# Sums of weights at a fixed place of each step, second weights ahead of first ones, one count of conversion pieces for each place

## The chip, the cores and the metric

One core of a Trainium2 chip runs the kernel. Times are device microseconds (us) of one launch. The engines are TensorE (PE; its weight loads are PEld), VectorE (DVE), ScalarE (ACT), GpSimd (POOL) and SyncE (SP), which issues the DMAs. Each engine runs its own instructions in order, and semaphores hold an instruction until what it needs is there.

## The reference, cut to what matters

Attention with a learned bias feeds two blocks of matrix products. The change lies in the second half of the first block:

```python
def _moe_ref(x, w_tok1, w_tok2, w_ch1, w_ch2):      # x: (4, 576, 512)
    xt = x.transpose(0, 2, 1)
    h = np.maximum(xt @ w_tok1, 0.0) @ w_tok2        # 576 -> 256 -> 576
    u = x + h.transpose(0, 2, 1)
    h2 = np.maximum(u @ w_ch1, 0.0) @ w_ch2          # 512 -> 1536 -> 512
    return (u + h2).astype(np.float32)
```

The second block has weights w_in (512 x 1024) and w_out (512 x 512). All these weights arrive as 64-bit floats.

## The kernel before, in words

The channel products `u @ w_ch1` and `h2 @ w_ch2` run over 2304 token columns. The 1536 hidden units are cut into 12 rows f of 128, and the rows into six pairs j. Weight row f of w_ch1 is called c1 f here (first weights), row f of w_ch2 is c2 f (second weights).

Two passes go over the columns, `d0` and `d1` (class `Double`), each over 1024 columns in two blocks of 512; `d0` takes the 256 columns left over with it (`up256`, `down256`). In a pass, `run` makes one step n for each pair j. A step does the first product by a scheme with seven small products in the place of eight: P1, b, S2, S1, S3, P4 and S4, of six matmuls each, some of which use sums of weights (`wsum`, tile ws). Then come the second products, `down`, 12 matmuls each. Products for the left block run in each step (`down1`), those of the right block only once a group of two pairs is through: a step with n = 2 or 4 "begins" a group, closes the last one (four adds to X, L1277) and runs four more `down` (in `other`). Two result buffers `gs` pass the hidden values from ACT (high part, L1111) and DVE (low part, L1115) to PE. Every operand is a pair of a high and a low part, and a product takes three matmuls: high by high, high by low, low by high.

Weights are brought into that form on the chip by a queue of jobs (class `Jobs`). A job takes a 512 KB weight tile in four pieces, each one DVE instruction (L161, L171, L179, L185), with one square on ACT (L158); a piece of the next job also issues the job's high part (ACT, L122) and low part (DVE, L132). SP loads the tile of the next job as a job starts; two tiles of raw weights are held. `work(k)` issues up to k pieces, as long as `wjobs.limit` allows it, and `step` calls `work`; these calls are the places. `wjobs.need(key)` issues all pieces that a weight still needs, at once. The sums are jobs too: ("raw", j) makes four differences (L989, two steps), ("sum", j) makes the high part (L992, ACT), the low part (L995, DVE), and stores tiles to DRAM for pass `d1` (`keep`).

Before, the queue holds for each j: c1 2j, c1 2j+1, raw j, sum j, c2 2j, c2 2j+1. In `d0` a place has 3 pieces (`pieces`), with none at the first two places of a step that begins; the limit rises at marked points (`hooks0`). The token products of the stage before `d0` have their own counts (TP0, TP1, TPD), 26 pieces in all. Behind the product b stands `wjobs.need(("sum", j))`; in front of `down256` stands `wjobs.need(("c2", f))`. At the start of `d0` pieces are issued until sum 1 is done.

All code is written in the order in which it is to run; nothing reorders it.

Of the kernel before, what the change touches and what calls it, by code (L numbers as in the profile page):

```python
# [19 lines left out]
def kernel(ctx, tc, ins, consts, out, dbg=None, nb=4, stop=None):  # L20
# [30 lines left out]
    NF = CH // P  # L51
# [876 lines left out]
    D1 = C256 + CS  # L928
# [48 lines left out]
    S1, S3, S4, S2 = range(4)  # L977
    summed, sum_room = set(), []

    def sum_steps(j):  # L980

        def w(f):
            t = wjobs.last["c1", f].rearrange("p (a b) -> p a b", a=ND)
            return t[:, 0:ND2], t[:, ND2:ND]

        raw = []

        def add(i, x, y, op=ALU.subtract):
            V.tensor_tensor(out=raw[0][:, i], in0=x, in1=y, op=op)  # L989

        def hi(o):
            S.copy(out=wsum[j][:, 0, o], in_=raw[0])  # L992

        def lo(o):
            V.tensor_tensor(out=wsum[j][:, 1, o], in0=raw[0], in1=wsum[j][:, 0, o].bitcast(F32), op=ALU.subtract)  # L995

        def sums(first, second):
            (a11, a12), (a21, a22) = w(2 * j), w(2 * j + 1)
            if first:
                add(0, a21, a22, ALU.add)  # L1000
                add(1, a11, a21)
            if second:
                k = len(raw[0].shape) and raw[0].shape[1] - 2
                add(k + 1, raw[0][:, 0], a11)
                add(k, a12, raw[0][:, k + 1])

        def kept_():
            wjobs.subtract()
            if j < NJ - 2:
                keep("a", j, wa[j])  # L1010
                keep("b", j, wb[j])

        def done():
            if j < NJ - 1:
                keep("s", j, wsum[j])
            summed.add(j)

        def small_one():
            wjobs.finish()
            new_s(j)  # L1020
            raw.append(stg.tile([P, WMAX], F32, tag="sq", name="sq").rearrange("p (o a b) -> p o a b", o=2, a=ND2))
            sums(True, False)
            hi(slice(0, 2))

        def small_two():
            lo(slice(0, 2))
            sums(False, True)
            hi(slice(2, 4))

        def small_three():  # L1030
            lo(slice(2, 4))
            done()

        def one():
            raw.append(sum_room[0].rearrange("p i (o a b) -> p (i o) a b", o=2, a=ND2))
            sums(True, False)

        def two():
            sums(False, True)

        def three():
            new_s(j)
            hi(slice(0, 4))

        def four():
            lo(slice(0, 4))
            done()

        if j == 0:
            return [lambda: None], [small_one, small_two, small_three, kept_]  # L1050
        if j == 1:
            return [one, two], [three, four, wjobs.finish, kept_]
        return [one, two], [wjobs.finish, three, kept_, four]

    def c1_jobs(j):
        for f, dst in ((2 * j, a_dst), (2 * j + 1, b_dst)):
            fs = slice(f * P, (f + 1) * P)
            wjobs.add(("c1", f), "moe_w_ch1", slice(0, DM), fs, ND, lambda dst=dst: dst(j))
        raws_, sums_ = sum_steps(j)
        wjobs.add_steps(("raw", j), raws_)  # L1060
        wjobs.add_steps(("sum", j), sums_)

    base = len(wjobs.queue)
    for j in range(NJ):
        c1_jobs(j)
        for f in (2 * j, 2 * j + 1):
            fs = slice(f * P, (f + 1) * P)
            wjobs.add(("c2", f), "moe_w_ch2", fs, slice(0, DM), 1, lambda f=f: [[t[:, :] for t in c2[f]]])
    wjobs.limit = base + 8
    wjobs.load()  # L1070

    def work(k):
        for _ in range(k):
            if wjobs.gen is not None or wjobs.next < min(len(wjobs.queue), wjobs.limit):
                wjobs.piece()
# [51 lines left out]
    if True:  # L1127
        TP0, TP1, TPD = 2, 1, (2, 2, 1, 1)
        M2, M1 = mixers
# [21 lines left out]
        for b in range(nb):  # L1151
            if b == nb - 1:
                u = u_parts(0, u0)
            if b > 0:
                h = new_h()
                work(TP0)
                for m in range(NTT):
                    if m == 1 and b + 1 < nb:
                        work(TP1)
                    ph = pk["h"].tile([P, DM], F32, tag="h", name="ph")  # L1160
                    tok1(xs, m, ph)
                    tok1_out(ph, m, h)
# [8 lines left out]
            for d in range(ND):  # L1171
# [6 lines left out]
                if b == nb - 1 and d == 2:  # L1178
                    x256 = chw.tile([P, 2, ND, CS], F32R, tag="ws1", name="x256")
                    split(X[:, :, C256:C256 + CS], x256[:, 0], x256[:, 1])  # L1180
                work(0 if b == nb - 1 else TPD[d])
    tk.release()
# [74 lines left out]
    with tc.tile_pool(name="ps_ch", bufs=1, space=PSUM, reuse_waits="tile") as pc:  # L1257
# [30 lines left out]

        def step(k):
            work(k)  # L1290
            rfill(1)
# [39 lines left out]
        class Double:  # L1331
# [29 lines left out]

            def other(self, acc, lst, k, n=0):
                down(acc, self.g(k), lst[k][0], k == 0, k == len(lst) - 1)
                if k + 2 < len(lst):
                    self.second(k + 2, lst)
                step(n)

# [26 lines left out]
            def run(self, hooks, first=False, small=False, banks=("ma", "ma", "mb", "mb"), end=None, fill=None):  # L1394
# [3 lines left out]
                for n, (group, j) in enumerate(seq):  # L1398
# [11 lines left out]
                    sm, da = small and n < len(seq) - 1, n > 0 and not (first and n == 1)  # L1410
                    k_ = self.pieces
                    k1 = 0 if begins and small else k_
                    a = bank(banks[n % 2])
                    product(a, self.half(w_a, 0), self.half(self.u, 0), start=True)
                    S.copy(out=s1, in_=a)
                    step(k1)
                    two = da and not sm and not begins
                    if da:
                        self.down1(pj, 0, pgrp, range(ND2) if two else range(ND))
                    step(k1)  # L1420
                    if begins:
# [11 lines left out]
                    hooks(n, "P2")  # L1433
                    wjobs.need(("sum", j))
                    product(a, ws_(S2), M2)
                    S.copy(out=c12, in_=a)
                    step(k_)
                    if two:
                        self.down1(pj, 0, pgrp, range(ND2, ND))
                        relu(s1, gs[0])  # L1440
                    if sm:
                        up256(j)
                        hooks(n, "up")
                        step(k_ if not begins else 1)
                        relu_lo_256()
                    if begins:
                        acc = new_acc()
                        self.other(acc, lst, 0, k_)
                        if not small:
                            self.other(acc, lst, 1, k_)  # L1450
                    c = bank(banks[3] if sm else "mx")
# [7 lines left out]
                    hooks(n, "P7")  # L1459
                    step(k_)  # L1460
                    if begins:
                        for k in range(1 if small else 2, len(lst)):
                            self.other(acc, lst, k, k_ if k + 1 < len(lst) else 0)
                            if not small and k == len(lst) - 2:
# [5 lines left out]
                    elif n > 0:  # L1470
                        self.down1(pj, 1, pgrp)
                        step(1)
                    elif fill is not None:
# [12 lines left out]
                    if not small:  # L1486
                        step(1)
                group, j = seq[-1]
# [7 lines left out]
                else:  # L1496
                    self.second(0, lst)
                    step(self.pieces)
                self.down1(j, 1, group)
# [4 lines left out]
                self.second(1, lst)  # L1504
                step(self.pieces)
                acc = [bank(nm) for nm in end] if end else new_acc()
                for k in range(len(lst) - 1):
                    self.other(acc, lst, k, self.pieces)
                    build()
# [29 lines left out]
        d1 = Double(D1, [order1[i:i + 2] for i in range(0, NJ, 2)])  # L1539
        d0.pieces, d1.pieces = 3, 0  # L1540
        scratch = rp_.tile([P, 2, DM], F32, tag="r", name="scratch")
# [5 lines left out]
        def hooks0(n, where):  # L1547
            if where == "start":
                wjobs.limit = base + 6 * (n + 1) + 1
                if n == 0:  # L1550
                    wjobs.limit = base + 10
                    while 1 not in summed:
                        wjobs.piece()
                    mixer(3, raws(), 0)
            if n == 1 and where == "P2":
                mixer(4, raws(), 0)
            if where == "up":
                wjobs.limit = base + 6 * (n + 1) + (3 if n > 0 else 4)
            if n == 0 and where == "others":
# [3 lines left out]
            if n == 0 and where == "C21":  # L1563
                work(2)
                mixer(1, slots[2:4], 0)
            if where == "P3":
                wjobs.limit = base + 6 * (n + 1) + 6
                work(4 if n > 0 else 0)
            if n < NJ - 1:
# [12 lines left out]
        def hooks1(n, where):  # L1582
# [10 lines left out]
            if where == "done":  # L1593
# [6 lines left out]
                wjobs.load()  # L1600
                d1.pieces = 2
            if n == NJ - 1 and where == "P4":
# [335 lines left out]
```

## Time and profile before

| | |
|---|---|
| median of 3 runs | 886.04 us (884.84 to 886.21) |
| the profiled execution | 884.93 us, span 883.1 us |
| PE busy | 853.7 us, 97% of the span |
| DVE busy | 696.8 us, 79% |
| ACT busy | 454.8 us, 51% |
| mean granted clock of PE | 0.988 |

Times within the trace count from the start of the span. The profiled execution takes 1.8 us more than its span. PE's busy time includes matmuls that run at a lower clock. In views by windows a row gives the stretch and its length, then the busy time and instruction count of PE, PEld, DVE, ACT and POOL, the granted clock of PE, the DMA share and GB/s. In views of waits a row gives who waited for whom, the total in us, how often, and the longest. In a timeline the bracket is the idle time before the instruction and what ended it.

### The profile page before, as it was taken

What the parts mean: (1) busy time and instruction counts of PE and PEld (TensorE: products, weight loads), DVE (VectorE), ACT (ScalarE), POOL (GpSimd) and SP (SyncE); (2) the same over time, 40 slices, a digit from 0 to 9 for tenths busy, and PEclk for the clock granted to TensorE, in tenths of its full rate; (3) what the DMA queues carried; (4) which work ended last, traced back from release to release, by engine and by line L of the source; (5) the groups of instructions that cost most, each with busy time, mean ns of one, the idle gap of its engine ahead of it and who ended that gap; (6) DMA issues with size and microseconds to landing.
All of it is one profiled execution on the core that took longest, in us unless ns stands there. A gap on an engine that the chain in (4) does not pass through costs nothing.

```text
span 883.1 us, 21618 instructions
## 1 busy us (share of the span) xinstructions
PE 853.7 (97%) x8608; PEld 708.4 (80%) x8608; DVE 696.8 (79%) x1521; ACT 454.8 (51%) x992; POOL 231.4 (26%) x440
## 2 busy tenths in 40 slices
PE   8999999999999999997897899999999999999998
PEld 4466788888888988886686778888878989989997
DVE  7899788888887778895785696556579889988756
ACT  7999888888888534442332343213244432323310
POOL 1345567666676100000000000000003332322230
PEclk9999999999999999998998999999999999999999
DMA  7966543444432132232341202326025001010002
GB/s 189 192 137 135 141 82 75 82 89 92 94 69 56 50 112 91 96 104 111 96 155 71 72 1 72 106 109 212 27 85 115 25 1 49 1 60 1 1 13 96
DMA packets 127733, 74.30 MB, mean 84 GB/s; under 512 B 104593, under 2 KB 112913, under 8 KB 126353
## 3 DMA queue, kind: packets, MB, share of 16 engines
q1 hardware_dynamic: 127472, 72.79, 31.4%
q8 instruction: 68, 1.11, 0.6%
q14 instruction: 33, 0.26, 0.1%
q10 hardware_dynamic: 160, 0.13, 0.1%
HBM read 47.01 MB, written 13.11 MB: 68 GB/s over the span
## 4 chain that ended last, share of the span: by engine, by line
PE 53%; DVE 8%; ACT 2%; issue 1%; DVEq 0%
PE a L1269 12%; PE ps L1749 6%; PE pu L1727 6%; PE po L1780 6%; PE pv L1674 6%; PE ma L1105 5%; PE mx L1105 2%; PE my L1105 2%; PE mb L1105 2%; PE mx L1301 2%; DVE X L1277 1%; PE ph L684 1%; PE pu L1140 1%; DVE g L1115 1%; PE mx L1322 1%; PE my L1322 1%
## 5 line engine op out<-in xcount | busy, mean ns | idle before, releaser
L540 POOL TENSOR_SCALAR pr<-pr,sm 128x576 f32<-128x576 f32 (+2 forms) x208 | 130.2, 643 | 45.9 <-DVE sm L533 37.7
L1269 PE MATMUL a<-g,c 128*128 128x512 f32 x528 | 125.9, 390 | 0.0
L1269 PEld LDWEIGHTS a<-g,c 128*128 128x128 f32 x528 | 98.6, 188 | 21.4 <-DVE g L1115 1.0
L526 ACT ACTIVATE pr<-pr,mn 128x576 f32<-128x576 f32 x144 | 112.2, 780 | 6.6 <-DVE mn L513 4.4
L513 DVE CUSTOM_DVE_ANT_0 pr<-ss,bias_m 128x576 f32<-128x576 f32 x128 | 94.5, 749 | 18.9 <-PE ss L507 17.1
L63 POOL TENSOR_TENSOR y<-X,y 128x576 fp32r<-128x576 f32 x4 | 6.6, 1690 | 375.4 <-DMA wsr<-in_moe_w_sg_dram 375.4
L607 PEld LDWEIGHTS o<-xA,vm 64*64 64x64 f32 x1280 | 69.8, 133 | 11.1 <-issue 5.4
L607 PE MATMUL o<-xA,vm 64*64 64x128 f32 (+1 forms) x1280 | 78.7, 261 | 0.0
L1224 DVE STREAM_TRANSPOSE res<-X 32x256 f32<-32x256 f32 (+1 forms) x176 | 68.2, 387 | 2.8
L608 PE MATMUL o<-yA,vm 64*64 64x128 f32 x1024 | 67.7, 272 | 0.0
L507 PE MATMUL ss<-kt,X 64*64 64x288 f32 x816 | 66.8, 410 | 0.0
L608 PEld LDWEIGHTS o<-yA,vm 64*64 64x64 f32 x1024 | 56.2, 133 | 0.4
L1749 PE MATMUL ps<-wsT,vn 128*128 128x288 f32 x384 | 56.5, 295 | 0.0
L384 DVE TENSOR_SCALAR X<-ttab,wsm 128x576 f32<-128x576 f32 x108 | 55.3, 572 | 0.1
L1749 PEld LDWEIGHTS ps<-wsT,vn 128*128 128x128 f32 x384 | 52.7, 188 | 0.5 <-DVE tmp L1757 0.2
L1727 PEld LDWEIGHTS pu<-y,c 128*128 128x128 f32 x384 | 51.3, 188 | 0.3
L1727 PE MATMUL pu<-y,c 128*128 128x288 f32 x384 | 51.5, 294 | 0.0
L583 PE MATMUL x<-ident,pr 128*128 128x128 f32 x320 | 47.0, 273 | 0.0
L1780 PE MATMUL po<-u,gm 128*128 128x512 f32 x192 | 44.0, 389 | 0.0
L158 ACT ACTIVATE sq<-wraw 128x512 f32<-128x512 f32 (+2 forms) x44 | 28.8, 654 | 28.8 <-DVE w L185 18.4
L1111 ACT ACTIVATE g<-cs 128x512 fp32r<-128x512 f32 x24 | 15.2, 632 | 52.6 <-PE a L1269 36.8
L63 POOL TENSOR_TENSOR gm<-uT,gm 128x512 fp32r<-128x512 f32 x16 | 23.7, 1482 | 69.8 <-ACT gm L62 69.8
(262 smaller groups left out, 2004.6 us busy)
## 6 DMA issues: line engine op xcount, KB each, us to landing
wraw<-in_moe_w_ch_dram SPq DMA_DIRECT2D x24, 512.0 KB, 3.5
bias_m<-bst SPq DMA_DIRECT2D x32, 288.0 KB, 3.9
s<-ws SPq DMA_DIRECT2D x5, 1024.0 KB, 4.2
ws<-s SPq DMA_DIRECT2D x5, 1024.0 KB, 5.2
vm<-in_v_dram SPq DMA_DIRECT2D x32, 128.0 KB, 3.3
wraw<-in_moe_w_in_dram SPq DMA_DIRECT2D x8, 512.0 KB, 4.9
out_dram<-res SPq DMA_DIRECT2D x16, 256.0 KB, 2.1
kr<-in_k_dram SPq DMA_DIRECT2D x48, 72.0 KB, 2.6
```

Of the source, the lines that this page charges most:

```text
L507: T.matmul(ss[a % na][o, hf, 0:HN], lhsT=ql, rhs=kr_, start=True, stop=True)
L513: V.tensor_tensor_reduce(out=pr[:, a * NB:a * NB + N].rearrange("p (f n) -> p f n", f=2), in0=ss[a][:, :, 0:HN], in1=bias[a].rearrange("p ...
L526: S.activation(out=pr[:, a * NB:a * NB + N], in_=pr[:, a * NB:a * NB + N], func=AF.Exp, scale=-1.0, bias=mn[:, a:a + 1], accum_out=sm[:, a ...
L540: G.tensor_scalar(out=pr[:, dc:dc + hi - lo], in0=pr[:, lo:hi], scalar1=sm[:, a:a + 1], scalar2=1.0, op0=ALU.mult, op1=ALU.mult,)
L607: T.matmul(o[0:HD, 0:w], lhsT=vm[r, t, 0], rhs=xs[r, t, 0:w], start=st_, stop=en)
L608: T.matmul(o[HD:P, 0:w], lhsT=vm[r, t, 1], rhs=rh[r], start=st_, stop=en)
L1105: T.matmul(ps, lhsT=w[i][:, d], rhs=x[j][:, d], start=start and d == 0 and n == 0, stop=stop and d == ND2 - 1 and n == 2, skip_group_check ...
L1224: V.transpose(out=o, in_=src(c)[32 * a:32 * a + 32])
L1269: T.matmul(acc[d], lhsT=c2[f][i][:, d * P:(d + 1) * P], rhs=g[:, j], start=start and m == 0, stop=stop and m == 2,)
L1727: T.matmul(pu[:, hf, 0:HN], lhsT=wi[i][0][d][:, f * P:(f + 1) * P], rhs=y[j][:, d, js], start=d == 0 and m == 0, stop=d == ND - 1 and m == 2,)
L1749: T.matmul(ps[:, hf, 0:HN], lhsT=vn[i][:, t, ds_], rhs=wsT[j][:, t, js], start=t == 0 and m == 0, stop=False,)
L1780: T.matmul(po[:, cs], lhsT=g[i][:, d, gs], rhs=wo[j][d][:, cs], start=d == 0 and m == 0, stop=d == NG - 1 and m == 2,)
```

## The change: what it does

It changes four things in the order of the instructions.

1. The queue. The jobs for c2 of pair j stand in front of those for c1 of pair j (from j = 1). "raw" remains a job; the job "sum" becomes "kept", which only finishes the low parts and stores them.
2. The sums. For n > 1 their high part is issued at a new hook behind P1 (behind ACT's copy s1), their low part and the store at a new hook behind the first `down1`. For j = 1 both come at the start of `d0`. `wjobs.need(("sum", j))` goes. For j = 0 they are part of the job "raw".
3. The counts. `work()` takes its count from a list of 115, one for each call. The places and their order stay. The list gives 30 pieces to the token stage, and pieces to the first two places of the steps that begin.
4. The limits follow the new order of the queue.

```diff
-        def three():
+        def whole():
             new_s(j)
             hi(slice(0, 4))

-        def four():
+        def rest_():
             lo(slice(0, 4))
             done()

         if j == 0:
-            return [lambda: None], [small_one, small_two, small_three, kept_]
-        if j == 1:
-            return [one, two], [three, four, wjobs.finish, kept_]
-        return [one, two], [wjobs.finish, three, kept_, four]
+            return [small_one, small_two, small_three], [kept_]
+        sums_of[j] = whole, rest_
+        return [one, two], [wjobs.finish, kept_]
...
     for j in range(NJ):
-        c1_jobs(j)
+        if j == 0:
+            c1_jobs(j)
         for f in (2 * j, 2 * j + 1):
             wjobs.add(("c2", f), ...)
+        if j > 0:
+            c1_jobs(j)
+    at = {job[0]: i + 1 for i, job in enumerate(wjobs.queue)}
-    wjobs.limit = base + 8
+    wjobs.limit = at["c1", 3]
...
-    def work(k):
-        for _ in range(k):
+    counts = [
+        2, 2, 1, 2, 1, 1, 2, 3, 1, 2, 2, 1, 3, 2, 1, 1, 2, 0, 1, 0, 0, 1, 0, 4,
+        3, 3, 3, 4, 1, 3, 2, 0, 3, 0, 4, 3, 3, 1, 0, 4, 1, 3, 6, 2, 3, 3, 3, 0,
+        2, 4, 0, 2, 3, 0, 2, 2, 6, 4, 0, 3, 4, 4, 1, 1, 4, 1, 6, 0, 0, 0, 0, 0,
+        1, 0, 0, 0, 0, 2, 0, 0, 0, 0, 0, 0, 0, 0, 0, 0, 4, 2, 3, 2, 0, 0, 0, 3,
+        2, 2, 2, 3, 2, 0, 0, 1, 1, 2, 4, 1, 1, 1, 1, 1, 2, 4, 1,
+    ]
+    def work():
+        for _ in range(counts.pop(0)):
             if wjobs.gen is not None or wjobs.next < min(len(wjobs.queue), wjobs.limit):
                 wjobs.piece()
...
                     S.copy(out=s1, in_=a)
-                    step(k1)
+                    hooks(n, "P1")
+                    step()
...
                         self.down1(pj, 0, pgrp, range(ND2) if two else range(ND))
-                    step(k1)
+                    hooks(n, "D1")
+                    step()
...
                     hooks(n, "P2")
-                    wjobs.need(("sum", j))
...
             if where == "start":
-                wjobs.limit = base + 6 * (n + 1) + 1
+                wjobs.limit = at["c1", min(2 * n + 2, NF - 2)]
                 if n == 0:
-                    wjobs.limit = base + 10
-                    while 1 not in summed:
-                        wjobs.piece()
+                    wjobs.limit = at["raw", 1]
+                    wjobs.need(("raw", 1))
+                    for f in sums_of[1]:
+                        f()
                     mixer(3, raws(), 0)
+            if n > 1 and where in ("P1", "D1"):
+                if where == "P1":
+                    wjobs.need(("raw", n))
+                sums_of[n][where == "D1"]()
...
             if where == "up":
-                wjobs.limit = base + 6 * (n + 1) + (3 if n > 0 else 4)
+                wjobs.limit = at["c1", 2 * n + 4] if 2 * n + 4 < NF else at["kept", NJ - 1]
...
             if where == "P3":
-                wjobs.limit = base + 6 * (n + 1) + 6
-                work(4 if n > 0 else 0)
+                work()
```

Every other `work(k)` and `step(k)` loses its argument in the same way.

## Rows read from the trace of the kernel before

**Rows 1.** The page, part 2: busy tenths in 40 slices.
```profile
PE   8999999999999999997897899999999999999998
...
PEclk9999999999999999998998999999999999999999
```

**Rows 2.** Waits of PE from 358 to 545 us.
```profile
PE ma L1105 <- DVE ws L995: 8.3, 2, 4.4
PE my L1322 <- DVE c L132: 3.5, 4, 1.6
PE my L1322 <- ACT c L122: 2.6, 4, 0.9
```

**Rows 3.** Busy time by windows: last token batch, then d0's steps 0 to 5.
```profile
342.93:358.61 15.68, 15.68 (x91) 13.94 (x89) 13.59 (x21) 8.85 (x15) 0.00 (x0) 1.00 0.11 34
358.61:377.43 18.82, 17.40 (x98) 14.80 (x97) 15.90 (x27) 8.77 (x15) 0.00 (x0) 1.00 0.35 127
377.43:396.10 18.67, 18.42 (x104) 15.68 (x103) 18.24 (x32) 9.31 (x18) 0.00 (x0) 1.00 0.33 92
396.10:442.03 45.93, 37.15 (x164) 30.12 (x163) 29.74 (x52) 11.72 (x21) 0.00 (x0) 0.89 0.31 106
442.03:462.96 20.93, 20.93 (x114) 18.25 (x115) 17.63 (x30) 8.46 (x14) 0.00 (x0) 1.00 0.49 164
462.96:509.96 47.00, 37.58 (x163) 30.19 (x161) 29.59 (x52) 12.39 (x22) 0.00 (x0) 0.89 0.20 67
509.96:525.05 15.09, 15.09 (x66) 12.50 (x67) 13.87 (x24) 8.19 (x14) 0.00 (x0) 1.00 0.01 1
```

**Rows 4.** Busy time by windows, behind the longest wait of step 2.
```profile
409.60:414.00 4.40, 4.37 (x16) 3.98 (x17) 2.40 (x4) 1.16 (x2) 0.00 (x0) 0.50 0.68 276
414.00:418.00 4.00, 4.00 (x25) 3.56 (x24) 0.69 (x1) 0.60 (x1) 0.00 (x0) 1.00 0.42 131
```

**Rows 5.** Timeline of step 2 around that wait.
```profile
404.09 0.69 DVE L1115 SCALAR_TENSOR_TENSOR g<-cs,g 128x512 fp32r<-128x512 f32 x1 [4.24 <-ACT g L1111]
...
404.70 2.48 DVE L1277 TENSOR_TENSOR X<-a,X 128x512 f32<-128x512 f32 x4
...
408.36 1.22 DVE L995 TENSOR_TENSOR ws<-scratch,ws 128x1024 fp32r<-128x1024 f32 x1
...
409.63 2.08 PE L1105 MATMUL ma<-m,ws 128*128 128x512 f32 x4 [4.43 <-DVE ws L995]
```

**Rows 6.** Groups by line from 285 to 540 us: busy, mean ns.
```profile
L179 DVE SCALAR_TENSOR_TENSOR w<-wraw,w 128x512 int32<-128x512 int32 x24 | 16.6, 690 | 0.7
...
L161 DVE TENSOR_SCALAR w<-wraw 128x512 int32<-128x512 int32 x24 | 10.1, 419 | 0.0
...
L132 DVE TENSOR_TENSOR c<-w,c 128x512 fp32r<-128x512 f32 x12 | 8.2, 686 | 1.7 <-ACT c L122 1.7
...
L995 DVE TENSOR_TENSOR ws<-scratch,ws 128x1024 fp32r<-128x1024 f32 x5 | 6.1, 1221 | 2.1 <-ACT ws L992 2.1
...
L992 ACT CAST ws<-scratch 128x1024 fp32r<-128x1024 f32 x5 | 5.2, 1048 | 17.8 <-issue 9.4 <-DVE scratch L989 8.4
```

**Rows 7.** Timeline at the start of d0.
```profile
364.92 1.05 ACT L992 CAST ws<-scratch 128x1024 fp32r<-128x1024 f32 x1 [8.44 <-DVE scratch L989]
...
369.12 0.59 ACT L1381 ACTIVATE cs<-ma 128x512 f32<-128x512 f32 x1
...
374.57 1.58 PE L1322 MATMUL my<-g,c 128*128 128x256 f32 x11 [0.53 <-DVE g L1115]
```

**Rows 8.** Timeline in the second token batch.
```profile
325.60 0.63 PE L668 MATMUL px<-ident,X 128*64 128x128 f32 x4 [1.61 <-DVE x L63]
```

**Rows 9.** The tile wraw from 285 to 540 us.
```profile
DMA to landing us min/median/max: 3.3/3.5/4.3
```

**Rows 10.** Timeline where d1 ends and the second block begins.
```profile
667.54 6.63 POOL L63 TENSOR_TENSOR y<-X,y 128x576 fp32r<-128x576 f32 x4 [375.43 <-DMA wsr<-in_moe_w_sg_dram]
...
667.72 1.93 DVE L132 TENSOR_TENSOR c<-w,c 128x512 fp32r<-128x512 f32 x1
```

More of the change, by code (lines that the diff above doesn't have):

```diff
@@ L977 @@
     S1, S3, S4, S2 = range(4)
-    summed, sum_room = set(), []
+    sums_of, sum_room = {}, []
     def sum_steps(j):
@@ L1015, in done @@
                 keep("s", j, wsum[j])
-            summed.add(j)
         def small_one():
@@ L1060, in c1_jobs @@
         wjobs.add_steps(("raw", j), raws_)
-        wjobs.add_steps(("sum", j), sums_)
+        wjobs.add_steps(("kept", j), sums_)
     base = len(wjobs.queue)
     for j in range(NJ):
-        c1_jobs(j)
+        if j == 0:
+            c1_jobs(j)
         for f in (2 * j, 2 * j + 1):
@@ L1127 @@
     if True:
-        TP0, TP1, TPD = 2, 1, (2, 2, 1, 1)
         M2, M1 = mixers
@@ L1155 @@
                 h = new_h()
-                work(TP0)
+                work()
                 for m in range(NTT):
                     if m == 1 and b + 1 < nb:
-                        work(TP1)
+                        work()
                     ph = pk["h"].tile([P, DM], F32, tag="h", name="ph")
@@ L1180 @@
                     split(X[:, :, C256:C256 + CS], x256[:, 0], x256[:, 1])
-                work(0 if b == nb - 1 else TPD[d])
+                work()
     tk.release()
@@ L1287, in relu, with step @@
             relu_lo(src, g)
-        def step(k):
-            work(k)
+        def step():
+            work()
             rfill(1)
@@ L1360, in g, with other @@
                 return gs[(k + self.small) % 2]
-            def other(self, acc, lst, k, n=0):
+            def other(self, acc, lst, k):
                 down(acc, self.g(k), lst[k][0], k == 0, k == len(lst) - 1)
@@ L1365, in other @@
                     self.second(k + 2, lst)
-                step(n)
+                step()
             def pair0(self):
@@ L1410, in run @@
                     sm, da = small and n < len(seq) - 1, n > 0 and not (first and n == 1)
-                    k_ = self.pieces
-                    k1 = 0 if begins and small else k_
                     a = bank(banks[n % 2])
@@ L1419, in run @@
                         self.down1(pj, 0, pgrp, range(ND2) if two else range(ND))
-                    step(k1)
+                    hooks(n, "D1")
+                    step()
                     if begins:
@@ L1433, in run @@
                     hooks(n, "P2")
-                    wjobs.need(("sum", j))
                     product(a, ws_(S2), M2)
                     S.copy(out=c12, in_=a)
-                    step(k_)
+                    step()
                     if two:
@@ L1443, in run @@
                         hooks(n, "up")
-                        step(k_ if not begins else 1)
+                        step()
                         relu_lo_256()
@@ L1447, in run @@
                         acc = new_acc()
-                        self.other(acc, lst, 0, k_)
+                        self.other(acc, lst, 0)
                         if not small:
-                            self.other(acc, lst, 1, k_)
+                            self.other(acc, lst, 1)
                     c = bank(banks[3] if sm else "mx")
@@ L1459, in run @@
                     hooks(n, "P7")
-                    step(k_)
+                    step()
                     if begins:
                         for k in range(1 if small else 2, len(lst)):
-                            self.other(acc, lst, k, k_ if k + 1 < len(lst) else 0)
+                            self.other(acc, lst, k)
                             if not small and k == len(lst) - 2:
@@ L1471, in run @@
                         self.down1(pj, 1, pgrp)
-                        step(1)
+                        step()
                     elif fill is not None:
@@ L1486, in run @@
                     if not small:
-                        step(1)
+                        step()
                 group, j = seq[-1]
@@ L1497, in run @@
                     self.second(0, lst)
-                    step(self.pieces)
+                    step()
                 self.down1(j, 1, group)
@@ L1504, in run @@
                 self.second(1, lst)
-                step(self.pieces)
+                step()
                 acc = [bank(nm) for nm in end] if end else new_acc()
                 for k in range(len(lst) - 1):
-                    self.other(acc, lst, k, self.pieces)
+                    self.other(acc, lst, k)
                     build()
@@ L1539 @@
         d1 = Double(D1, [order1[i:i + 2] for i in range(0, NJ, 2)])
-        d0.pieces, d1.pieces = 3, 0
         scratch = rp_.tile([P, 2, DM], F32, tag="r", name="scratch")
@@ L1563, in hooks0 @@
             if n == 0 and where == "C21":
-                work(2)
+                wjobs.limit = at["c1", 4]
+                work()
                 mixer(1, slots[2:4], 0)
             if where == "P3":
-                wjobs.limit = base + 6 * (n + 1) + 6
-                work(4 if n > 0 else 0)
+                work()
             if n < NJ - 1:
@@ L1600, in hooks1 @@
                 wjobs.load()
-                d1.pieces = 2
             if n == NJ - 1 and where == "P4":
```

## Prediction

> **What bounds the kernel now.** I read the page first: PE is busy nearly throughout, and the two dips in its slices are also the only ones in its clock [rows 1]. Then the waits of PE over the pass d0: the sums of weights (ws, L995) and the second weights (c, from L132 and L122) head them, and each of the largest falls in two places only [rows 2]. Then windows cut at the starts of d0's steps [rows 3]. The reader is to see there that steps 3 and 5 are PE from end to end, at full clock, while steps 2 and 4, which begin a group, take 45.93 and 47.00 us at a clock of 0.89.
>
> What would those two take without a wait? Step 5 is 66 matmuls of 512 columns in 15.09 us, 0.229 us each. Step 3 is 20.93 us. A beginning step is step 3 and four more `down` of 12 matmuls: 20.93 + 48 x 0.229 = 31.9 us. So step 2 loses 14.0 us and step 4 15.1 us, 29.1 us in all. That is the most that these steps can give back.
>
> The timeline of step 2 shows how [rows 5]. The first two places of a beginning step have no pieces, so DVE sits idle for 4.24 us; then the low part g, four adds to X and last the low part of the sums go through its queue, and PE waits 4.43 us at S2. [...] Later in the same step `down256` finds its c2 weights unconverted; all that is left of them is issued in front of it.
>
> **The new order, counted.** The queue, the limits and the counts of the diff fix which piece falls on which place, and so do those of the kernel before. Counted out, two things follow. No `need` has to force a piece inside d0 any more; before, the sums of pairs 2 and 4 and five second weights were forced. And the DVE work that each step issues (instructions by their durations: a conversion 0.42 + 3 x 0.69, a low part 0.69, the low sum 1.22 [rows 6], an add to X 0.62 [rows 5]) becomes: step 0 17.0 to 18.6 us, step 1 21.8 to 23.5, step 2 29.8 to 29.0, step 3 20.4 to 21.7, step 4 29.8 to 28.6, step 5 13.8 to 7.4. The count for step 2 before, 29.8, stands against 29.74 us of DVE in its window [rows 3]. DVE instructions that don't depend on each other follow at about 0.62 (four adds in 2.48 us), so the work of steps 2 and 4 fits in 31.9 us of PE, with little over.
>
> **Steps 2 and 4: the sums.** ACT's high sum costs 1.05 us and stands behind the copy s1, at P1's end; DVE's low sum costs 1.22 us. Counted from the start of step 2: P1 ends at 1.4; DVE still has the tail of step 1 (two adds, g, c12, two differences, two low parts, two pieces) until 5.0, then the low sum until 6.1. S2 comes after P1, 24 matmuls of `down1` and b, at 8.4. The sum is there 2.3 us early. What is queued behind it on DVE, the first g of the group, isn't wanted before `down1` ends at 7.0. [...]
>
> **Steps 2 and 4: the second weights.** With c2 in front of c1, c2 4 and 5 are converted in step 1 and c2 8 and 9 in step 3. The waits for c of `down256`, 6.1 us in eight pieces [rows 2], go, and so do the slow matmuls behind them.
>
> **What is late next there.** DVE's queue in step 2, followed instruction by instruction: behind `down256` the second g reaches PE at 21.9, PE wants it at 21.15; the low parts of s1 and a come behind the four closing adds, and the next P1, which writes the bank that a's low part reads, waits until 33.5 instead of 32.6; the low part of s1 at the start is 0.2 late. That is 1.8 us, so step 2 takes 31.9 + 1.8 = 33.7. Step 4 has fewer pieces behind `down256` (2 + 3 instead of 4 + 3), and the same sum gives 0.8: 32.7. Gains: 45.9 - 33.7 = 12.2 and 47.0 - 32.7 = 14.3, together 26.5 us. Bounds: 29.1 with no wait left; 15 if PE's waits are only halved.
>
> **The start of d0 pays.** All of c1 2, c1 3 and the sums of pair 1 must be through before the mixers. Before, c1 3's first piece was done in the token stage; now, because c2 2 and 3 go first, the start of d0 has the low part of c2 3, two more pieces of c1 2 and the first of c1 3 on top: 0.69 + 0.69 + 0.69 + 0.42 = 2.5 us, and one more piece of 0.69 stands in the last token batch. DVE is the chain there: ACT's high sum waits for it, ACT's copy cs, which frees a PSUM bank for PE's next product, stands behind the mixer's parts in ACT's queue, and PE waits for g at `down256` [rows 7]. So nearly all of 3.2 us lands on PE, mostly as one wait before the product c. Step 1 issues 1.7 us more (two differences and a piece come forward), of which some 1.4 reach PE through g. The token stage gives back 0.6: the sums' second half moves ahead of the x split for which PE waited 1.61 us [rows 8], but four more pieces fill DVE's 2.1 us of idle time in a batch [rows 3]. Sum for start and token stage: 3.2 + 1.4 - 0.6 = 4.0. Bounds: 1.4, if step 0 catches up on ACT's waits (8.44 us before the high sum [rows 7]), to 7.
>
> The wait of about 3 us raises one question more. [...] 3.2 is nearer to 4.43, so I count a stretch like that of rows 4: it slows c by some 2 us, of which DVE's chain hides half. 1.0 us. Bounds 0 to 2.2.
>
> [...]
>
> **Loads.** SP loads a tile once the raw buffer two jobs back is read; 3.3 to 4.3 us to landing [rows 9] against 2.9 us of DVE for a job and its low part. Only in step 3, with six pieces at one place, is there a chance of a wait, under 1 us, and DVE has slack there: 0. Step 3 stays at 20.9. Step 5: its low sum is 0.3 late for S2: 0.3. The tail of d0 has the same work: 0.
>
> **d1 and the second block.** PE is the bound in d1. At its end four pieces come later; two DVE instructions already take longer there while POOL splits y (1.93 instead of 0.69 [rows 10]). ACT's y stands behind the last high part, so POOL starts later too. I take 0.5 us; bounds 0 to 2.5 (two instructions at 1.24 us more each).
>
> **Sum.** -26.5 + 4.0 + 1.0 + 0.3 + 0.5 = -20.7 us. The profiled execution took 884.93, which makes 864.2; it lies 1.1 below the median of 886.04, so the forecast for the median is 865.3, said as 865.
>
> **The rivals.**
> *DVE stays the bound in the beginning steps.* 29 us of DVE in 32 of PE, much of it waiting for PE in turn: if each g is late and a wait of 4 us comes back in each step, with its slow stretch, half the gain goes: 865 + 13 = 878. For it: DVE's queue is in order and g stands behind pieces. Against it: step 3 has 20.4 us of DVE in 20.93 and PE doesn't wait [rows 3].
> *The start costs more.* 7 + 2.2 instead of 4.0 + 1.0: 869.5. [...]
> *The start costs nothing much* (1.4, no stretch) and steps 2 and 4 reach the floor: 865.3 - 3.6 - 2.6 = 859.
> *Slower: conversions outrun their loads.* Now pieces come in runs of four and six and p1 of the next job waits in DVE's queue, with g and the adds behind it. There are 16 such jobs in d0. It decides from 20.7 / 16 = 1.3 us of wait for each on; at 1.6 the kernel takes 891. Against it: nothing on DVE waited for raw weights before, landing is 4.3 at most [rows 9], and the load goes out a job ahead.
> *The change doesn't do what it says:* high sums held on ACT by the store of the sums before them. That store goes out a whole step earlier, so I give this no case of its own.
>
> **How the numbers follow.** Forecast 865 (862 to 868): 0.60. More at the start, 869.5: 0.15. Better, 859: 0.10. Half the gain, 878: 0.11. Slower: 0.03; no change: 0.01. Changes within 0.2% (1.8 us) are about what a measurement here can't tell from none. Faster 0.96. The range 859 to 872 leaves out the last three and little else, 0.17.
>
> **What would show it.** No wait of PE for L995, none for c; steps 2 and 4 at 33 to 35 us and full clock; a new wait of some 3 us before the product c in step 0, and step 2 starting 4 to 5 us later than 396.1. The forecast is wrong if PE's waits for g (L1115) exceed 4 us in a beginning step, or if a dip of the clock remains in steps 2 or 4.

## The result, and the profile after

| | before | after |
|---|---|---|
| median | 885.44 us (883.93 to 886.21, 4 runs) | 861.69 us (861.57 to 864.17, 4 runs) |
| profiled execution, span | 884.93, 883.1 us | 861.75, 859.7 us |
| mean granted clock of PE | 0.988 | 0.997 |

The medians differ by 23.75 us. The ratio, taken from the means, is 0.9741 (0.9718 to 0.9763). The forecast of 865 was 3.3 us too high.

The same two lines of the page as in [rows 1]: the dips of steps 2 and 4 are gone, from PE and from its clock. The last slice is an 8 in both; the one other 8 left is the slice of step 0.

```profile
PE   9999999999999999989999999999999999999998
...
PEclk9999999999999999999999999999999999999999
```

Waits of PE from 358 to 545 us, beside [rows 2]. No wait for ws is left and none for c; one for ACT's copy cs, in step 0, is new.

```profile
PE ma L1116 <- ACT cs L1391: 2.9, 1, 2.9
PE ma L1116 <- DVE g L1126: 0.7, 2, 0.6
PE ma L1116 <- ACT cs L1445: 0.7, 1, 0.7
PE a L1279 <- DVE g L1126: 0.3, 1, 0.3
```

The windows of [rows 3]: the last token batch, then steps 0 to 5.

```profile
342.45:358.49 16.04, 15.98 (x91) 13.86 (x89) 13.84 (x21) 8.64 (x15) 0.00 (x0) 1.00 0.12 34
358.49:380.29 21.80, 18.82 (x99) 15.87 (x97) 18.34 (x30) 10.15 (x17) 0.00 (x0) 0.92 0.34 121
380.29:400.27 19.98, 18.72 (x104) 15.68 (x103) 19.52 (x36) 9.28 (x18) 0.00 (x0) 1.00 0.38 107
400.27:433.16 32.89, 32.46 (x163) 26.92 (x163) 27.61 (x48) 11.70 (x20) 0.00 (x0) 1.00 0.42 142
433.16:454.06 20.90, 20.90 (x115) 18.25 (x116) 19.81 (x37) 8.99 (x16) 0.00 (x0) 1.00 0.50 166
454.06:486.16 32.10, 31.97 (x164) 26.89 (x162) 26.32 (x45) 11.69 (x21) 0.00 (x0) 1.00 0.20 66
486.16:501.25 15.09, 15.09 (x66) 12.45 (x67) 8.80 (x16) 6.01 (x10) 0.00 (x0) 1.00 0.01 1
```

Column by column against before: steps 0 and 1 are 2.98 and 1.31 us longer, steps 2 and 4 are 13.04 and 14.90 shorter and at full clock, steps 3 and 5 as they were. With the token stage's 0.12 that makes 23.8 us by 501.25. The start of d0 in the timeline, beside [rows 7]:

```profile
371.98 0.59 ACT L1391 ACTIVATE cs<-ma 128x512 f32<-128x512 f32 x1
...
372.62 2.02 PE L1116 MATMUL ma<-u,wq 128*128 128x512 f32 x6 [2.90 <-ACT cs L1391]
374.44 2.76 PE L1116 MATMUL ma<-u,wb 128*128 128x512 f32 x6
...
376.70 0.68 DVE L1126 SCALAR_TENSOR_TENSOR g<-mx,g 128x512 fp32r<-128x512 f32 x1
```

The copy that frees the bank ma comes 2.9 us too late, and the product behind it takes 4.4 us (372.62 to 377.00) instead of the 2.7 of twelve such matmuls at full clock (0.229 us each). The clock there, by windows; the first two mix stretches at a granted clock of 1.00 and of 0.50 (0.50 throughout from 374.2 to 376.4):

```profile
373.50:375.50 2.00, 2.00 (x7) 1.57 (x6) 0.51 (x2) 2.00 (x4) 0.00 (x0) 0.56 0.64 252
375.50:377.50 2.00, 1.91 (x6) 1.18 (x5) 1.88 (x3) 1.24 (x3) 0.00 (x0) 0.59 0.00 0
377.50:379.50 2.00, 2.00 (x17) 2.00 (x18) 1.63 (x3) 1.24 (x4) 0.00 (x0) 1.00 0.00 0
```

The end of d1, beside [rows 10]:

```profile
646.49 6.80 POOL L63 TENSOR_TENSOR y<-X,y 128x576 fp32r<-128x576 f32 x4 [354.07 <-DMA wsr<-in_moe_w_sg_dram]
...
646.81 1.93 DVE L185 SCALAR_TENSOR_TENSOR w<-sq,w 128x512 f32<-128x512 f32 x1
...
674.72 0.40 PE L1761 MATMUL ps<-wsT,vn 128*128 128x288 f32 x1 [0.94 <-POOL vn L63]
```

Before, POOL began with y 2.82 us ahead of the second block's first product (667.54 against 670.36); now it begins 0.64 behind it (645.85), and 28 us later PE waits 0.94 for POOL's vn.

### The profile page after: what moved, and what is told of

It reads as the page before. It is cut to its first block, busy times and chain, and to the rows that moved or that the text cites. A ratio compares the mean times of both kernels' runs of the same rounds, so it can differ in the third digit from the quotient of the medians.

```text
span 859.7 us, 21623 instructions
## 1 busy us (share of the span) xinstructions
PE 846.1 (98%) x8608; PEld 702.7 (82%) x8608; DVE 693.5 (81%) x1521; ACT 454.5 (53%) x991; POOL 230.9 (27%) x440
## 4 chain that ended last, share of the span: by engine, by line
PE 79%; DVE 14%; ACT 2%; issue 2%; DMA 1%; POOL 1%; SPq 0%; DVEq 0%; ACTq 0%
PE a L1279 11%; PE ss L507 9%; PE ps L1761 6%; PE po L1792 6%; PE o L607 5%; PE ma L1116 4%; PE pu L1739 4%; PE pv L1686 4%; PE x L583 4%; PE y L588 3%; PE bps L403 3%; PE o L608 2%; PE mx L1116 2%; PE mb L1116 2%; PE my L1116 2%
## 5 line engine op out<-in xcount | busy, mean ns | idle before, releaser
L1792 PEld LDWEIGHTS po<-u,gm 128*128 128x128 f32 x192 | 36.0, 188 | 7.4
```

What stands on the lines that cost most here:

```text
L1792: T.matmul(po[:, cs], lhsT=g[i][:, d, gs], rhs=wo[j][d][:, cs], start=d == 0 and m == 0, stop=d == NG - 1 and m == 2,)
```

## The experiments

Lengths of the steps in us, each from the first product P1 of one step to that of the next, in the profiled execution of each kernel:

| kernel | step 0 | 1 | 2 | 3 | 4 | sum | median (range), ratio to before |
|---|---|---|---|---|---|---|---|
| before | 18.82 | 18.67 | 45.93 | 20.93 | 47.00 | 151.35 | |
| after | 21.80 | 19.98 | 32.89 | 20.90 | 32.10 | 127.67 | 861.69, 0.9741 |
| e1 | 18.83 | 18.67 | 39.05 | 21.07 | 37.25 | 134.87 | 871.51 (871.32 to 872.16), 0.9846 (0.9832 to 0.9861) |
| e2 | 24.78 | 19.63 | 40.89 | 22.52 | 41.97 | 149.79 | 886.38 (884.88 to 887.92), 1.0008 (0.9997 to 1.0019) |
| e3 | 25.05 | 19.29 | 34.26 | 20.89 | 33.94 | 133.43 | 867.01 (865.87 to 867.33), 0.9795 (0.9779 to 0.9812) |
| e4 | 21.84 | 19.61 | 39.45 | 23.84 | 38.02 | 142.76 | 878.56 (878.26 to 878.69), 0.9924 (0.9909 to 0.9939) |
| e5 | 23.06 | 18.86 | 32.86 | 20.90 | 32.10 | 127.78 | 861.29 (861.27 to 861.98), 0.9731 (0.9716 to 0.9745) |
| e6 | 17.83 | 22.24 | 32.88 | 20.90 | 32.10 | 125.95 | 859.83 (859.39 to 860.37), 0.9712 (0.9698 to 0.9727) |
| e7 | 21.80 | 19.97 | 32.87 | 20.90 | 32.10 | 127.64 | 861.25 (861.10 to 861.95), 0.9730 (0.9714 to 0.9746) |
| e8 | 18.82 | 18.66 | 33.84 | 20.90 | 32.32 | 124.54 | 859.31 (858.81 to 859.74), 0.9706 (0.9692 to 0.9721) |
| e9 | 16.70 | 22.62 | 33.82 | 20.89 | 32.32 | 126.35 | 859.93 (859.51 to 860.51), 0.9721 (0.9708 to 0.9734) |
| e10 | 18.82 | 18.67 | 37.43 | 20.89 | 35.06 | 130.87 | 865.13 (863.81 to 866.34), 0.9779 (0.9766 to 0.9793) |
| e11 | 18.82 | 18.66 | 34.47 | 20.89 | 33.06 | 125.90 | 860.56 (859.75 to 860.87), 0.9723 (0.9710 to 0.9737) |

**e1, the sums alone.** The kernel before with the hooks at P1 and D1 and without the `need`:

```diff
+            if n > 1 and where in ("P1", "D1"):
+                if where == "P1":
+                    wjobs.need(("raw", n))
+                sums_of[n][where == "D1"]()
...
-                    wjobs.need(("sum", j))
```

The two hooks themselves, and the sums of pair 1 at the start of `d0`, are as in the changed kernel.

> The kernel before with the sums at their fixed places alone; the queue (first weights ahead of second ones) and the counts stay. Theory (one queue, DVE's, makes both waits, so they stand in for each other): the waits for ws go, but PE then reaches down256 about 6.6 us earlier in steps 2 and 4 while the second weights in front of it are through only 2.0 us earlier (the low sum, 1.22, and two low parts of 0.42), so the waits for c grow to some 5 us a step and more; the kernel gains 3 to 7 us: 878 to 882. Rival (two separate waits, each with its own half-clock stretch): the ws waits of 8.3 us and their two stretches of 2.2 go and nothing comes back: 872 to 874.

The theory fell and the rival held; 871.5 is even a little under its 872 to 874. Steps 2 and 4 are 6.9 and 9.8 us shorter, and the waits for c are what they were (PE's waits from 340 to 560 us; the 1.0 for ws is in step 5):

```profile
PE my L1320 <- DVE c L132: 3.1, 4, 1.5
PE my L1320 <- ACT c L122: 2.6, 4, 0.9
PE ma L1103 <- DVE g L1113: 2.5, 2, 1.3
PE ma L1103 <- DVE ws L995: 1.0, 1, 1.0
```

Why, two rows of DVE in step 2 show, first of the kernel before, then of e1. The second weights stand behind these two parts g, and each part waits for a product of PE (through ACT). What held PE held DVE too; take PE's wait away and DVE moves up with it: the first part starts 20.2 us into step 2 before and 14.2 us in e1.

```profile
416.32 0.69 DVE L1115 SCALAR_TENSOR_TENSOR g<-mx,g 128x512 fp32r<-128x512 f32 x1 [2.68 <-ACT g L1111]
419.10 0.69 DVE L1115 SCALAR_TENSOR_TENSOR g<-cs,g 128x512 fp32r<-128x512 f32 x1 [2.09 <-ACT g L1111]
```

```profile
412.07 0.68 DVE L1113 SCALAR_TENSOR_TENSOR g<-mx,g 128x512 fp32r<-128x512 f32 x1
414.23 0.69 DVE L1113 SCALAR_TENSOR_TENSOR g<-cs,g 128x512 fp32r<-128x512 f32 x1 [1.47 <-ACT g L1109]
```

**e2, the queue alone.** c2 in front of c1, the sums a job as before, old counts:

```diff
-        c1_jobs(j)
+        if j == 0:
+            c1_jobs(j)
         for f in (2 * j, 2 * j + 1):
             wjobs.add(("c2", f), ...)
+        if j > 0:
+            c1_jobs(j)
...
```

The limits follow the new order here too.

> The kernel before with the second weights in front of the first ones alone; the sums stay a job that is finished behind the product b, the counts stay. Theory: the waits for c go; the waits for ws in steps 2 and 4 stay at about 4.4 us each, with half-clock matmuls behind them, and step 0 pays the 4.2 us that the new order showed there; steps 2 and 4 at about 39 us each: some 10 us gained, 875 (871 to 879). Rival (separate waits, and most of the gain is the sums'): the c waits of 6.1 us go and the start costs 4: 883 to 885.

No gain: the theory was wrong by 11 us, and the rival, nearer to it, still had the start too cheap. The c waits are gone and steps 2 and 4 are 10.1 us shorter together, but step 0 is 6.0 longer, step 1 1.0 and step 3 1.6; the 1.6 us that the steps still gain doesn't show in the median (PE's waits from 340 to 560 us):

```profile
PE ma L1109 <- DVE ws L995: 7.7, 2, 4.4
PE ma L1109 <- ACT cs L1385: 5.9, 1, 5.9
PE ma L1109 <- DVE g L1119: 4.0, 2, 2.0
```

The theory had the start at 4.2 us, the price in the kernel with the new counts, and had no waits for g.

**e3, sums and queue with the old counts.** The changed kernel with `work(k)` as before: 3 pieces a place, none at the first two of a step that begins, 26 in the token stage.

> The changed kernel (fixed sums, new queue) with the counts of the kernel before: 3 pieces a place in d0, none at the first two places of a step that begins, 26 in the token stage. Theory: the list only shares out work that fits anyway: 863 to 866, steps 2 and 4 within 1.5 us of 32.9 and 32.1, and the token stage's four pieces fall on the start of d0. Rival (the counts are what makes the work fit): g or c late again in steps 2 and 4, 870 or more.

867.0, between the two: the list is worth 5.3 us. One part is the start: PE waits 5.3 us there instead of 2.9, some four pieces of 0.6 more, those that the list puts into the token stage; steps 0 and 1 together are 2.6 us longer. The other part is the rival's: at the ends of steps 2 and 4 PE waits 2.0 us each for g, and these steps are 1.4 and 1.8 longer. It is the larger one, for the four pieces cost something in the token stage too: from the second-last batch's first matmul to step 0 the stage takes 30.43 us here (326.82 to 357.25) and 31.53 after (326.96 to 358.49).

```profile
PE ma L1115 <- ACT cs L1391: 5.3, 1, 5.3
PE ma L1115 <- DVE g L1125: 4.0, 2, 2.0
```

**e4, the sums one place later.** In the changed kernel:

```diff
-            if n > 1 and where in ("P1", "D1"):
-                if where == "P1":
+            if n > 1 and where in ("D1", "P2"):
+                if where == "D1":
                     wjobs.need(("raw", n))
-                sums_of[n][where == "D1"]()
+                sums_of[n][where == "P2"]()
```

> The changed kernel with both hooks of the sums one place later: the high part behind down1, the low part behind the product b, where DVE has g, four adds to X and the add to s1 in front of it. Theory (the place of the low sum in DVE's queue is the cause): PE waits for L995 again, about 2.9 us in steps 2 and 4 and 1.9 us in steps 3 and 5, and the clock dips behind the longer ones: 874 (870 to 878). Rival (with the new queue and counts DVE has slack and the place no longer matters): within 2 us of the changed kernel's 861.7.

16.9 us lost, a little over the theory's range: the place of the low sum is what made that wait (PE's waits from 340 to 560 us).

```profile
PE ma L1116 <- DVE ws L995: 10.5, 4, 3.8
```

**e5 and e6, step 0 in another order.** e5 issues the sums of pair 1 and mixer 3 behind pair 0's first two products, so that ACT's copies cs come first; e6 also puts mixer 2 behind the relu of c:

```diff
             if where == "start":
...
-                    for f in sums_of[1]:
-                        f()
-                    mixer(3, raws(), 0)
             if n == 0 and where == "others":
+                for f in sums_of[1]:
+                    f()
+                mixer(3, raws(), 0)
-                for i in range(2):                                   # e6 alone
-                    S.copy(out=M22[i], in_=M2[i].bitcast(F32))
-                mixer(2, raws(), 0)
             if n == 0 and where == "C21":
+                for i in range(2):
+                    S.copy(out=M22[i], in_=M2[i].bitcast(F32))
+                mixer(2, raws(), 0)
```

> The changed kernel with the sums of pair 1 and mixer 3 issued behind the first two products of step 0, so that ACT's two copies cs stand ahead of the high sum in ACT's queue; DVE's order is the same. Theory (step 0 is bound by DVE, and ACT's copies only pass that on): the wait of 2.9 us before the product c goes, but the low part of g for down256 still ends at about 376.5 in DVE's order, so PE waits some 4 us there instead; 860 to 862, against 861.7. Rival (the order of ACT's queue alone makes the wait): step 0 gets back the 2.9 us and the slow matmuls behind it, 857 to 858.5.

> As the last one, and mixer 2 (with the copy of M2) behind the relu of c, so that DVE's low part g for down256 no longer stands behind mixer 2. Theory: step 0 ends 3 to 4 us earlier, at about 376.5; the DVE work is the same and step 1 has 23.5 us of it in 18.7 us of PE, so about half comes back there as waits for g or for the copies c12: 858 to 860. Rival A (order was all): everything is kept, 857 to 858. Rival B (steps 0 to 2 are DVE's sum, whatever the order): 861 to 862.

Both theories held. In e5 the wait before c is gone and stands two products further on, with the slow matmuls behind it (the second row takes 2.71 us, 1.6 at full clock); steps 0 and 1 take 41.9 us together, as after (41.8). ACT's copy was mostly passing on DVE's lateness. Its order had a share: the low part g for `down256` ends 18.9 us into step 0 after and 17.9 in e5, because DVE waits 1.49 us for a copy of ACT's (tile m) there after and 0.51 in e5. Slower matmuls use that up.

```profile
375.70 0.58 PE L1332 MATMUL my<-g,c 128*128 128x256 f32 x1 [3.08 <-ACT g L1122]
376.62 2.71 PE L1332 MATMUL my<-g,c 128*128 128x256 f32 x11 [0.34 <-DVE g L1126]
```

In e6 step 0 is 4.0 us shorter and step 1 2.3 longer: 1.7 us stay.

**e7, the counts at the end of d1 as before.**

```diff
-        2, 2, 2, 3, 2, 0, 0, 1, 1, 2, 4, 1, 1, 1, 1, 1, 2, 4, 1,
+        2, 2, 2, 3, 2, 0, 1, 2, 2, 2, 2, 1, 1, 2, 2, 2, 2, 2, 0,
```

> The changed kernel with the last thirteen counts, those of the end of d1, as they fall in the kernel before. Theory (the list leaves too much for the last two places of d1, so the split of y on POOL starts 3.5 us later than before and the parts vn come late): the wait of 0.9 us for vn goes, the wait of 0.4 us for g comes back: 861.0, a gain of 0.5. Rival (vn is late because d0 ended earlier and something else now paces POOL): the 0.9 us stay, 861.7 or more.

The wait for vn goes and the one for g (0.41 us) is back, as the theory had it; the median is 0.4 us lower, inside what the runs can tell.

**e8, the old queue, with pieces at the empty places.** e1 and three counts:

```diff
...
-                    k1 = 0 if begins and small else k_
+                    k1 = k_
...
-                    step(k1)
+                    step(k1 + 1 if begins and small else k1)
...
-                        step(k_ if not begins else 1)
+                        step(k_ if not begins else 2)
```

> The kernel before with the sums at their fixed places and the old queue (first weights ahead), but with pieces at the first two places of the steps that begin: 3 and 4 instead of none, and 2 instead of 1 behind up256. Theory (the second weights came late because two places stood empty, not because of their place in the queue): c is ready in time in steps 2 and 4, these take 32.5 to 34 us, and step 0 stays at its 18.8 us, as in the kernel before: 859 to 863, as good as the changed kernel. Rival (the new queue is needed, the old one leaves too much work for the steps that begin): waits for c or g stay, 867 or more.

The theory held. Steps 0 and 1 cost what they cost before, steps 2 and 4 are nearly as short as after, and 859.3 is the lowest of all kernels here. On the same chip e7, which is the changed kernel but for its tail, took 861.25: what it has beyond e8 costs 1.9 us. That is the new queue with its list of counts, and pair 0's sums in the token stage. In the steps, 0 and 1 take 4.3 us more in e7 than in e8, and 2 and 4 take 1.2 less. No run separates the queue from its list here.

```profile
358.96:377.78 18.82, 17.42 (x99) 14.80 (x97) 15.91 (x27) 8.77 (x15) 0.00 (x0) 1.00 0.34 127
...
396.44:430.28 33.84, 32.58 (x163) 26.86 (x162) 30.45 (x54) 11.83 (x22) 0.00 (x0) 1.00 0.44 144
```

**e9, e8 with e6's order of step 0 and the sums of pair 0 ahead of their store.**

> The kernel e8_old_queue_pieces with two things more: step 0 in the order of e6_mixer_later (ACT's copies cs first, mixer 2 behind the relu of c), and the sums of pair 0 ahead of the store of their low parts, as in the changed kernel, so that PE's wait of 1.6 us for x falls to 0.3. Theory: 1.3 us from the token stage, and half of step 0's 1.4 us of waits: 857 to 858. Rival (both come back as waits later in steps 1 and 2): 859 or more.

The rival: nothing kept. Step 0 falls to 16.70, PE from end to end, and step 1 rises to 22.62, where PE now waits for ACT's copies: 1.8 us for s (first row) and 0.6 for cs, with a granted clock of 0.83 in the 2 us behind the first and 0.92 over the step. The second row is in step 2.

```profile
PE ma L1103 <- ACT s L1413: 1.8, 1, 1.8
PE my L1320 <- DVE g L1113: 1.2, 1, 1.2
```

**e10 and e11, counts alone.** The kernel before, with its queue and its sums as a job. e11 changes the two empty places and nothing else:

```diff
-                    k1 = 0 if begins and small else k_
+                    k1 = k_
...
-                    step(k1)
+                    step(7 if begins and small else k1)
```

e10 has 8 there, and 2 instead of 1 behind `up256`.

> The kernel before with three counts changed and nothing else: 3 pieces at the first place and 8 at the second of steps 2 and 4 instead of none, and 2 instead of 1 behind up256. The sums stay a job in the queue; these pieces reach them there, so that their low part stands ahead of g and of the four adds. Theory (the two empty places were the whole cause, and neither the hook for the sums nor the new queue is needed): 859 to 863. Rival (the fixed place is needed: a need or a late low sum stays somewhere in d0): 866 or more.

> The kernel before with the counts of the first two places of steps 2 and 4 alone changed: 3 and 7 instead of none; the place behind up256 keeps its 1. Against e10_counts_only that is one piece less in front of the first g and two less in front of the g for down256. Theory (what e10 still lost, 2.0 us of wait for g in each of these steps, is pieces issued too early and standing in front of g in DVE's queue): the waits for g in down256 halve, 862 to 863.5, within 4 us of e8_old_queue_pieces with neither hook nor new queue. Rival (the sums as a job in the queue are what costs: low sum and stores at the wrong place): 864.5 or more, as e10.

e10 lands between its theory and its rival. It puts so many pieces ahead that the first g of the group waits behind them until 410.51, and one of them for its raw weights (timeline of e10, step 2):

```profile
410.17 0.43 DVE L161 TENSOR_SCALAR w<-wraw 128x512 int32<-128x512 int32 x1 [0.47 <-DMA wraw<-in_moe_w_ch_dram]
410.51 0.68 DVE L1115 SCALAR_TENSOR_TENSOR g<-cs,g 128x512 fp32r<-128x512 f32 x1
```

e11, two pieces less, is at 860.56, better than its theory. Its waits of PE from 350 to 560 us are all short, none for ws and none for c, and the ratio lies inside the interval of the changed kernel: two counts give the whole gain.

```profile
PE my L1322 <- DVE g L1115: 2.8, 3, 1.5
PE my L1322 <- ACT g L1111: 0.8, 1, 0.8
```

## Why the prediction was right, point by point

The measured 861.69 lies inside 859 to 872, but 0.3 us under the band of 862 to 868 that got a chance of 0.60: the mechanism was right, and most terms were a little too dear.

**Steps 2 and 4, the sums.** Right: no wait for L995, and a granted clock of 1.00. The low sum ends 6.0 us into step 2 (405.05 + 1.22 - 400.27), 6.1 were counted. e4 shows the place of the low sum as the cause, and e1 that moving it is worth 14.1 us alone.

**Steps 2 and 4, the second weights.** Right: no wait for c. The steps came out at 32.89 and 32.10, a little below the 33 to 35 that were to show it.

**The DVE work.** The count is a sum of durations, and it was compared with the trace for step 2 alone (29.8 and 29.74). Step 3 before has 17.63 us in its window [rows 3], not 20.4, and step 1 18.24, not 21.8; after, no step but 5 has as much as was counted (step 2: 27.61, not 29.0). So step 3 before was not as tight as the argument against the first rival had it. The conclusion held: the work of steps 2 and 4 fits.

**What is late next there.** The right waits, sized too high. 2.6 us were counted over the floor of 63.8; 1.2 were measured (32.89 + 32.10). The late second g of step 2 is a wait of 0.3 at `down` where 0.8 was counted, and the next P1 waits 0.2 instead of 0.9. Gain 27.9 instead of 26.5.

**The start of d0.** Step 0 paid 2.98 and step 1 1.31, against 3.2 and 1.4 counted, as one wait before c and smaller ones in step 1 (0.6 for g, 0.7 for a copy of ACT's). e5 and e6 confirm that DVE's work is most of the chain there; ACT's order has a share of about 1 us.

**The stretch at a lower clock.** It came: behind a wait of 2.9 us the granted clock was 0.56 to 0.59 for 4 us. It cost PE 1.7 us in the product c. The 1.0 us on the path was wrong: at full clock c would have ended earlier and `down256` would have waited for its g, which DVE ends at 377.4; from 364 to there nothing on DVE waits for PE. e4, which leaves step 0 as it is, shows a piece of this. Its matmuls slowed later, the first six of c took 1.68 us instead of 2.02, c took 4.04 instead of 4.38, PE then waited 0.33 for g, and step 0 kept its 21.8. No run has c wholly at full clock behind that wait.

```profile
377.02 1.61 PE L1332 MATMUL my<-g,c 128*128 128x256 f32 x11 [0.33 <-DVE g L1126]
```

That the stretch was counted at all was partly luck. The choice went by the length of the wait, 1.61 us with a granted clock of 1.00 behind it against 4.43 us with 0.50 [rows 4]; the same wait of 1.61 us was followed by a dip in other executions (last section).

**Token stage.** PE's wait for x fell from 1.6 [rows 8] to 0.3, but the four pieces took 1.1 (e3): 0.1 gained, not 0.6. **Step 5:** 0 instead of 0.3. **Loads:** one wait of DVE for raw weights in d0, 0.42 us in step 3, hidden (step 3 takes 20.90).

**The end.** 0.5 counted, 0.4 measured, but from another mechanism: 0.7 gained in d1 and 1.1 lost behind it. Not DVE beside POOL (one slow instruction, of 1.93 us, instead of two, of 1.93 and 1.91), but POOL's own late start, which shows at vn. e7 confirms it.

**The offset.** 1.1 us were added because the profiled execution lay below its median. After, the two agree (861.75 and 861.69), so here the addition was wrong. With the 1.4 of steps 2 and 4, 0.3 in steps 0 and 1, 1.0 for the clock, 0.3 in step 5 and 0.1 at the end, less 0.5 in the token stage, that is 3.7 us; rounding (865.3 to 865) and 0.2 us more around the span than before take it to the 3.3 us of the miss, within 0.1.

**The rivals.** DVE didn't stay the bound in steps 2 and 4, and the start didn't cost more. Conversions did outrun a load, once in the changed kernel (0.42 us) and for longer in others, in step 3 each time: 3.15 us in e1, 2.63 in e3, 2.43 in e4. In e1 and e3 that cost PE next to nothing, step 3 took 21.07 and 20.89 us; e10 has two such waits, 0.47 and 0.43, in steps 2 and 4. What no rival asked is whether all parts of the change were needed: the new queue earns nothing alone (e2), the kernel with it is 1.9 us behind e8, and the hook is replaced by two counts (e11). Work at the empty places ahead of DVE's idle 4.24 us [rows 5] takes both waits away by itself; moving the sums (e1) or the second weights (e2) takes away one each, 16.6 and 10.1 us in steps 2 and 4, against 27.9 for the whole change.

What stays open is how far e8 lies below the changed kernel: their intervals overlap, and the 1.9 us are from e7. Nor was a version tried that takes steps 0 and 1 below the sum of 37.5 us that they have in e8; e9 shows that an order alone doesn't.

## What to carry to other kernels

Where PE waits behind an in-order engine, look first at where that engine stands idle just ahead of the late instruction, and give that place work; a reordered queue moves the load elsewhere, and here (e2) its start and step 3 cost most of what it earned. Two late products in one queue need not stand in for each other: if the engine that makes them waits for PE in turn, both waits go one by one, and an experiment with one part alone tells. Before a wait is ordered away, ask what is late next: in step 0 three orders moved the same DVE work about, and at most 1.7 us of it was gained.

## What the runs showed of the hardware

Waits of the same length on PE were followed by different clocks. In the token stage the kernels before and e1 run the same instructions up to a wait of 1.61 us for x. The twelve matmuls behind it took 1.86 us before and 3.06 in e1:

```profile
326.26 1.86 PE L1140 MATMUL pu<-t,h 128*128 128x288 f32 x12
...
326.55 3.06 PE L1138 MATMUL pu<-t,h 128*128 128x288 f32 x12
```

From 328 to 330 us the granted clock was 1.00 before and 0.50 in e1, and from that wait to step 0 e1 took 34.5 us, before 33.0. Of the other kernels with this wait e2 and e10 dip behind it (the same twelve matmuls take 2.80 and 3.12 us), e8 and e11 don't (1.87 us in e8; e11's mean granted clock is 1.000). So a profile of one execution shows a stretch of some 1.5 us, or its absence, that the order of instructions alone doesn't decide. The changed kernel waits 0.3 us there and shows no dip (1.00 from 325 to 330 us).

In e10 these two rows of `down256` are the same eleven matmuls of steps 2 and 4: behind a wait of 2.02 us they take 2.36 us, behind one of 2.03 they take 1.58.

```profile
418.44 2.36 PE L1322 MATMUL my<-g,c 128*128 128x256 f32 x11 [2.02 <-DVE g L1115]
...
475.33 1.58 PE L1322 MATMUL my<-g,c 128*128 128x256 f32 x11 [2.03 <-DVE g L1115]
```

The granted clock by windows says the same, 0.60 and 1.00:

```profile
418.40:420.80 2.40, 2.36 (x12) 2.37 (x13) 2.38 (x4) 0.09 (x1) 0.00 (x0) 0.60 0.28 38
...
475.30:477.70 2.40, 2.37 (x19) 2.37 (x20) 2.38 (x4) 0.08 (x1) 0.00 (x0) 1.00 0.17 50
```

In step 2 of e10 PE had also waited 1.12 us (for `other`, until 411.94), 4.5 us before the longer wait began; in step 4 not. Whether that counts is not shown: in the token stage no other wait stands ahead, and the clocks differ all the same. In e5, behind 3.08 and 0.34 us, the granted clock was 0.50 for 5.9 us, from 375.7 to 381.6.
